# RWKV attention and a routed expert layer: attention by steps of 64 tokens on quarters of the array

## The chip, the cores and the metric

The kernel runs on one core of a Trainium2 chip. A core has a matrix engine (PE, whose weight loads are listed apart as PEld), a vector engine (DVE), a scalar engine (ACT), a general engine (POOL) and an engine that issues transfers (SP). Each runs its own stream of instructions in order, and they meet at semaphores. 16 DMA engines move data between HBM and the core's memory SBUF; PE writes its results to PSUM, 8 banks of 512 fp32 numbers in each of 128 partitions. The metric is the time of one execution in microseconds on the device; the median of three runs counts.

## The reference

Two blocks in a row. First an attention with a decaying state, for 4 batches, 8 heads, 768 tokens, 48 numbers per head:

```python
for t in range(S):
    kt, vt, rt = (k[:, :, t], v[:, :, t], r[:, :, t])
    cur = np.einsum('bhd,bhe->bhde', u[None] * kt, vt)
    y[:, :, t] = np.einsum('bhd,bhde->bhe', rt, state + cur)
    state = w[None, :, :, None] * state + np.einsum('bhd,bhe->bhde', kt, vt)
```

The term with `u` is a token's own term: the sum over d of r, u and k of this token, times v. Its outputs, laid side by side, are rows x of 384 numbers. Then a mixture of experts: 9 logits per token (8 experts and one gate that says whether the token keeps the expert of the token before it), and for each token one expert of 384 x 1024 x 384 with a relu between, scaled by the softmax's probability. All of it is in fp32.

## The kernel before

The attention works on 16 items; an item is one batch and one pair of heads (`M = B * HP`). Head 0 of the pair lies in partitions 0 to 47, head 1 in 64 to 111. The tokens of an item are cut into 6 chunks of 128 (`NCH`). Within a chunk the decay is moved into r and k: `rw` is r times a rising power of w, `kw` is k times the inverse power, so that their product gives the weights between tokens of a chunk. From chunk to chunk a state is carried.

Per item these steps are written, and each engine takes its part of them in this order (method `run`, lines 343 to 472):

- `load` (193): SP issues three transfers, `rk` (r and k turned, 768 KB), `kv` (k and v by tokens, 584 KB) and `vT` (v turned, 384 KB). They are issued three items ahead, each when its buffer is free.
- `scale` (207), on POOL: `ke` (k weighed for the chunk's end, two instructions), `rw` (two) and `pd` (r times k, two). `keys` (235), on DVE: `kw`.
- `scores` (273): 24 products, weights `kw` of 64 tokens of one head, moving `rw` of 128 or 64 tokens, into a pair of PSUM banks; DVE multiplies them with a mask into `am` (288), in two halves.
- `own` (260): 4 products of 384 columns with `u` as weights sum `pd` over d into `y`; DVE multiplies by `vT` in place (271).
- `added` (244): 10 products of all 128 tokens of a chunk into `T`, one per chunk and head. `states` (253): one scan on DVE over `T` gives the states.
- `inside` (290) and `before` (299), for the item before: 12 products with v as weights and `am` moving, and 10 with the state as weights and `rw` moving, added to `y`. The outputs have d along the partitions, so ACT copies them to `xT` (312) and `turn` (315) turns them: 6 transposes on PE and two ACT copies to `x`, which goes to HBM once per batch (326).
- `logits` (328) and `token_logits` (337), once per batch: 8 products of 384 columns from `xT`, then 3 that bring tokens to the partitions.

The first three items are written in an order of their own. From item 8 on (`g`) the router of the first two batches is spread over the items; item 15 issues the first gathers of rows for the experts. Then `Experts.run` (1274 on) takes over: `hidden` (1061) is the first product of the experts, and from there on PE runs the 10 blocks of rows. The first expert's weights are fetched by SP during item 14.

A product in fp32 is recorded twice in the trace, a pass each, and each pass has a weight load of its own. PE's four quarters (upper or lower half of the partitions in, upper or lower half out) can hold products of their own.

Of the kernel before, what the change touches and what calls it, by code (L numbers as in the profile page):

```python
# [1 line left out]

# [9 lines left out]
F32 = mybir.dt.float32  # L12
# [37 lines left out]
C2 = NCH // 2  # L50
AHEAD = 4
VB = NCH * 2 * DH

# [7 lines left out]
class Attention:  # L61
# [12 lines left out]

    def __init__(self, tc, st, rk_d, kv_d, vT_d, x_d, w_t, wp_d, kept, ident, lt, mp):
        self.tc, self.nc = tc, tc.nc
        nc = tc.nc
        self.rk_d, self.kv_d, self.vT_d, self.x_d = rk_d, kv_d, vT_d, x_d
        self.w_t, self.kept, self.ident, self.lt = w_t, kept, ident, lt

        self.late = st.enter_context(tc.tile_pool(name="late", bufs=1))
        self.wp = self.late.tile([P, H, 32], F32, name="wp")
        self.sel = self.late.tile([P, 2 * (E + 1)], F32, name="sel")
# [13 lines left out]
        self.T = mp[:, 2 * P + 2:2 * P + 2 + (NCH - 1) * DH].rearrange("p (e c) -> p e c", c=NCH - 1)  # L97

        self.inv = pool("pinv", 1, space=PSUM).tile([P, HP, P], F32, name="inv")
# [3 lines left out]
        self.rks, self.vTs = [None] * AHEAD, [None] * AHEAD  # L103
        for i in range(1, AHEAD + 1):
            self.rks[(n + i) % AHEAD] = once.tile([P, 2, NCH, P], F32, name=f"rk{i}")
        for i in range(1, AHEAD + 1):
            self.vTs[(n + i) % AHEAD] = once.tile([P, 2, C2, P], F32, name=f"vT{i}")
        self.kvs = [once.tile([P, 2 * VB + DP - DH], F32, name=f"kv{i}") for i in range(AHEAD + 1)]
        self.items = [dict() for _ in range(B * HP)]
        self.xTs, self.xs, self.lTs = {}, {}, {}  # L110
        for i in range(AHEAD - 1):
            self.load(i)
        nc.sync.dma_start(out=self.wp, in_=wp_d)


        self.step = once.tile([P, HP, DH, NCH - 1], F32, name="step")
        nc.vector.memset(self.step, 0.0)


        self.tab = tab = once.tile([P, HP, 2, P + 1], F32, name="tab")  # L120
# [8 lines left out]
        while n <= P:  # L129
            m = min(n - 1, P + 1 - n)  # L130
            for engine, t in ((nc.vector, tab[:, :1]), (nc.gpsimd, tab[:, 1:])):
                engine.tensor_mul(t[..., n:n + m], t[..., 1:1 + m], t[..., n - 1:n].to_broadcast([P, t.shape[1], 2, m]))
            n += m

        self.first, self.newton = mp[:, :P + 1], mp[:, P + 1:2 * P + 1]
        nc.scalar.copy(self.first, tab[:, 0, 0])
        self.reciprocals(0)

        self.end = once.tile([P, HP, P + DP], F32, name="end")
        self.endT = once.tile([P, 2, HP, 2 * DH], F32, name="endT")  # L140
# [12 lines left out]
    def reciprocals(self, i):  # L153

        nc, inv = self.nc, self.tab[:, i, 1, 1:]
        nc.vector.scalar_tensor_tensor(self.newton, self.first[:, 1:], -1.0, inv, Alu.mult, Alu.mult)
        nc.vector.scalar_tensor_tensor(self.inv[:, i], self.newton, 2.0, inv, Alu.add, Alu.mult)

# [6 lines left out]
    def ends(self, z):  # L165
        self.nc.scalar.copy(self.end[:, z, :P], self.tab[:, z, 0, P - 1::-1])
        self.nc.scalar.copy(self.end[:, z, P:], self.tab[:, z, 0, P - 1:DP - 1:-1])  # L167

    def turn_ends(self, z):
        ep, n = self.banks("ep"), z.stop - z.start  # L170
        for k in range(n):
            for o in range(2):
                self.nc.tensor.transpose(ep[:, o, k * P:(k + 1) * P], self.end[:, z.start + k, o * DP:o * DP + P], self.ident)
        self.nc.scalar.copy(self.endT[:, :, z].rearrange("p o i (h d) -> p o (i h) d", h=2),
                            ep[:, :, :n * P].rearrange("p o (i d) -> p o i d", d=DP)[..., :DH])

    def tables(self):

        nc, tab = self.nc, self.tab
        self.ends(slice(1, HP))  # L180
        for i in range(HP):
            nc.scalar.copy(self.step[:, i, :, 1:], spread(tab[:, i, 0, P:].to_broadcast([P, NCH - 2]), 1, DH))

    def chooser(self):

        self.nc.vector.tensor_reduce(self.sel, self.ident.rearrange("p (j i) -> p i j", j=4)[:, :2 * (E + 1)], axis=AX.X, op=Alu.add)
# [6 lines left out]
    def load(self, n):  # L193
        nc = self.nc
        b, hp = divmod(n, HP)
        rk, vT, kv = self.rks[n % AHEAD], self.vTs[n % AHEAD], self.kvs[n % (AHEAD + 1)]
        if n:
            nc.sync.dma_start(out=rk.rearrange("p a c t -> p (a c t)"), in_=self.rk_d[b, hp])
        else:
            for z in (slice(0, C2), slice(C2, NCH)):  # L200
                nc.sync.dma_start(out=rk[:, :, z], in_=self.rk_d[b, hp].rearrange("p (a c t) -> p a c t", a=2, c=NCH)[:, :, z])
        nc.sync.dma_start(out=kv, in_=self.kv_d[b, hp])
        nc.sync.dma_start(out=vT.rearrange("p a c t -> p (a c t)"), in_=self.vT_d[b, hp])
        self.items[n].update(b=b, hp=hp, rT=rk[:, 0], kT=rk[:, 1], vT=vT,
                             k=kv[:, :VB].rearrange("p (c x) -> p c x", c=NCH), v=kv[:, VB:])

    def scale(self, n):

        nc, t = self.nc, self.items[n]
        t["ke"] = self.two.tile([P, NCH, 2 * DH], F32, name="ke")  # L210
        t["pd"] = self.two.tile([P, NCH, P], F32, name="pd")
        t["rw"] = self.three.tile([P, NCH, P], F32, name="rw")
        hp = t["hp"]

        def ke(p):
            nc.gpsimd.tensor_mul(t["ke"][:, p::2], t["k"][:, p::2], spread(self.endT[:, p, hp], 1, C2))  # L216

        def pd(i):
            z = slice(i * C2, (i + 1) * C2)
            nc.gpsimd.tensor_mul(t["pd"][:, z], t["rT"][:, z], t["kT"][:, z])  # L220

        def rw(i):
            self.decayed(nc.gpsimd, n, slice(i * C2, (i + 1) * C2))

# [1302 lines left out]
```

## Time and profile before

| | us |
|---|---|
| median of 3 runs | 399.98 (399.34 to 401.64) |
| profiled execution | 398.36 |
| its span | 396.57 |
| first expert product (L1061) starts at | 119.34 |
| PE / PEld busy | 382.4 / 298.0 |
| DVE / POOL / ACT busy | 190.4 / 144.5 / 81.1 |
| data by SP's queue q1 | 56.89 MB |

The table of slices shows PE at 90% or more in nearly every fortieth of the span, a granted clock of full speed, and the DMA engines at 90% or more in the first six slices (60 us), at some 410 GB/s. "Issue" in the lists of waits is time in which an engine stood still and nothing that the profile shows held it. A stretch line gives for each engine the busy time and in brackets the number of instructions, in the order PE, PEld, DVE, ACT, POOL, then granted clock, DMA share and GB/s. A queue line gives packets, MB, and the share of the 16 engines' time.

### The profile page before, as it was taken

How to read it: one execution, taken by the hardware profiler on the slowest of the kernel's cores; microseconds unless marked ns; L12 is line 12 of the kernel's file. 1: busy time of each engine (PE TensorE's matmuls, PEld its weight loads, DVE VectorE, ACT ScalarE, POOL GpSimd, SP SyncE). 2: the span in 40 equal slices, each digit the busy share in tenths (PEclk: the TensorE clock that was granted, in tenths of full speed). 3: DMA queues.
4: the chain of work that ended last, by engine and by line, in shares of the span. 5: the costliest groups of instructions: out<-in, count | busy, mean ns of one | idle time of the engine just before them, and what ended most of it. 6: DMA issues, size and time to landing. Idle time of an engine off the chain costs nothing. (4 is left out here: it accounts for less than half of the span.)

```text
span 396.6 us, 8820 instructions
## 1 busy us (share of the span) xinstructions
PE 382.4 (96%) x3616; PEld 298.0 (75%) x3616; DVE 190.4 (48%) x533; ACT 81.1 (20%) x195; POOL 144.5 (36%) x179
## 2 busy tenths in 40 slices
PE   7999999999999999999999999999999999999992
PEld 6777777786769998666777787777767767779971
DVE  7887575778844743553432353255244244230200
ACT  4132222222222111111311121130031030131110
POOL 8679998887140052001633034014013023020012
PEclk9999999999999999999999999999999999999998
DMA  7999997998026774600842182073165064072011
GB/s 251 412 412 406 411 395 260 366 313 352 10 61 222 295 310 124 260 1 21 304 176 65 21 321 88 10 262 136 34 218 193 2 231 169 2 275 95 2 36 35
DMA packets 17473, 74.94 MB, mean 189 GB/s; under 512 B 2735, under 2 KB 6592, under 8 KB 14865
## 3 DMA queue, kind: packets, MB, share of 16 engines
q1 hardware_dynamic: 10048, 56.89, 38.5%
q0 software_dynamic: 3424, 9.54, 7.3%
q10 hardware_dynamic: 3952, 7.87, 5.3%
q8 instruction: 30, 0.49, 0.5%
q14 instruction: 19, 0.15, 0.1%
HBM read 64.85 MB, written 9.54 MB: 188 GB/s over the span
## 5 line engine op out<-in xcount | busy, mean ns | idle before, releaser
L1061 PE MATMUL h<-exT,w1t 128*128 128x192 f32 (+7 forms) x480 | 137.3, 428 | 1.0 <-ACT hT L1066 1.0
L1061 PEld LDWEIGHTS h<-exT,w1t 128*128 128x128 f32 x480 | 85.9, 190 | 33.9 <-issue 13.1
L1177 POOL DMA_INDIRECT out_dram<-yo,sid x27 | 27.6, 1021 | 183.2 <-ACT yo L1172 104.1
L1048 DVE COPY exT<-tp 128x384 f32<-128x384 f32 (+7 forms) x29 | 14.2, 494 | 96.6 <-PE tp L1047 96.6
L1066 ACT ACTIVATE hT<-h 128x192 f32<-128x192 f32 (+6 forms) x64 | 27.3, 428 | 142.6 <-PE h L1061 136.2
L1034 POOL DMA_INDIRECT xg<-x_d,gid x29 | 30.1, 1037 | 45.7 <-DVE sm L873 25.8
L288 DVE TENSOR_TENSOR am<-pair,kept 128x768 f32<-128x768 f32 x32 | 30.1, 952 | 16.3 <-PE pair L286 15.7
L220 POOL TENSOR_TENSOR pd<-rk 128x384 f32<-128x384 f32 x32 | 31.7, 1010 | 3.3 <-DMA rk<-in_rk_dram 2.5
L1074 PE MATMUL y<-hT,w2t 128*128 128x192 f32 (+1 forms) x144 | 29.1, 339 | 0.0
L295 PE MATMUL y<-am,kv 128*64 128x128 f32 x384 | 27.8, 278 | 1.1 <-DVE y L271 0.6
L1106 PE MATMUL y<-factors,sums 128*128 128x192 f32 x144 | 27.3, 326 | 0.0
L216 POOL TENSOR_TENSOR ke<-kv,endT 128x288 f32<-128x288 f32 x32 | 24.9, 796 | 4.6 <-DMA kv<-in_kv_dram 3.5
L233 POOL TENSOR_TENSOR rw<-rk,tab 128x384 f32<-128x384 f32 x26 | 23.5, 923 | 6.1 <-PE y L308 6.1
L295 PEld LDWEIGHTS y<-am,kv 128*64 128x64 f32 x384 | 23.9, 136 | 2.2 <-DVE y L271 1.2
L1074 PEld LDWEIGHTS y<-hT,w2t 128*128 128x128 f32 x144 | 25.0, 190 | 0.5
L1106 PEld LDWEIGHTS y<-factors,sums 128*128 128x128 f32 x144 | 24.1, 190 | 0.0
L286 PE MATMUL pair<-rw,kw 48*64 48x128 f32 (+1 forms) x768 | 22.5, 248 | 1.0 <-ACT end L167 0.6
L286 PEld LDWEIGHTS pair<-rw,kw 48*64 48x64 f32 x768 | 19.4, 133 | 2.4 <-ACT end L167 0.8
L312 ACT COPY xT<-y 128x768 f32<-128x768 f32 (+1 forms) x16 | 12.5, 779 | 40.9 <-PE y L308 40.9
L1113 PE MATMUL tp<-w2t,hT 128*120 128x384 f32 (+2 forms) x48 | 19.6, 490 | 0.0
L1106 PE MATMUL y<-w2t,hT 128*128 128x192 f32 x80 | 19.5, 326 | 0.0
L1106 PEld LDWEIGHTS y<-w2t,hT 128*128 128x128 f32 x80 | 14.2, 190 | 7.0 <-issue 2.7
(255 smaller groups left out, 496.5 us busy)
## 6 DMA issues: line engine op xcount, KB each, us to landing
w1t<-in_w_dram SPq DMA_DIRECT2D x9, 1536.0 KB, 6.2
w2t<-in_w_dram SPq DMA_DIRECT2D x9, 1536.0 KB, 8.9
rk<-in_rk_dram SPq DMA_DIRECT2D x15, 768.0 KB, 9.5
kv<-in_kv_dram SPq DMA_DIRECT2D x16, 584.0 KB, 9.9
vT<-in_vT_dram SPq DMA_DIRECT2D x16, 384.0 KB, 8.3
x_d<-x ACTq DMA_DIRECT2D x4, 1152.0 KB, 9.7
w1t<-in_w_dram ACTq DMA_DIRECT2D x1, 1536.0 KB, 9.3
w2t<-in_w_dram ACTq DMA_DIRECT2D x1, 1536.0 KB, 12.6
```

Source lines behind the costliest of these rows:

```text
L216: nc.gpsimd.tensor_mul(t["ke"][:, p::2], t["k"][:, p::2], spread(self.endT[:, p, hp], 1, C2))
L220: nc.gpsimd.tensor_mul(t["pd"][:, z], t["rT"][:, z], t["kT"][:, z])
L233: engine.tensor_mul(t["rw"][:, z], t["rT"][:, z], spread(pw, 1, z.stop - z.start))
L286: nc.tensor.matmul(sc[f * DP:(f + 1) * DP, h, i, x:], lhsT=t["kw"][q, c, o * DP:(o + 1) * DP], rhs=t["rw"][q, c, x:], start=True, stop=True)
L288: return lambda: nc.vector.tensor_mul(t["am"][:, g], sc, spread(self.kept[:, g:g + 3], 1, 2))
L295: nc.tensor.matmul(t["y"][p * DP:(p + 1) * DP, h, c2 * P:(c2 + 1) * P], lhsT=t["v"][:, (2 * c + h) * DH:(2 * c + h) * DH + DP], rhs=t["am" ...
L1034: self.nc.gpsimd.indirect_dma_start(out=xg[:n], out_offset=None, in_=self.x_d[:rows], in_offset=bass.IndirectOffsetOnAxis(ap=u["gid"][:n, ...
L1061: nc.tensor.matmul(h[:, :n], lhsT=u["w1"][:, m, kk, :], rhs=u["xT"][:, kk, :], start=(kk == 0), stop=(kk == DK - 1))
L1066: nc.scalar.activation(u[m], h[:, :n], Act.Relu)
L1074: nc.tensor.matmul(u["y"][d][:, :n], lhsT=u["w2"][:, m, d * P:(d + 1) * P], rhs=u[m], start=(m == 0), stop=(m == FK - 1))
L1106: nc.tensor.matmul(bank[:, x * half:(x + 1) * half], lhsT=a, rhs=b, start=(j == 0 and x == 0), stop=(j == FK // 2 - 1), skip_group_check=True)
L1177: self.nc.gpsimd.indirect_dma_start(out=out.rearrange("n (h d) -> (n h) d", h=2) if half else out, out_offset=bass.IndirectOffsetOnAxis(ap ...
```

## The change

The step becomes 64 tokens (`L`), so the state is carried 12 times per item, and every product of the attention is 64 by 64 in one quarter of the array (`quarter`). The own term is no longer a sum over `pd`: ACT multiplies k by u (`weighed`), PE forms all products of r and u k of a step (`own_terms`), and DVE keeps the diagonal in `am`; the weights between tokens of a step are then copied over it where a mask allows (`scores`, one predicated copy). `vT` and `pd` are gone. `added` makes a contribution for each of the 64-token steps; the first step is weighed for the end of the second (`k0`, `end0`), so that one scan of 480 elements carries 10 states, and ACT forms the one after the first step (`second`). `inside` and `before` now have `am` and `rw` as weights and v and the state (48 columns) moving, so that outputs have tokens along the partitions and ACT copies them straight to `x`. Two generators are drawn from in turn (`together`), so that the products of `added` of one item alternate with those of `inside` of the item before. Between `inside` and `before` ACT reads one column of `y` (`between`), which orders the two. `turn` now makes `xT` from `x`, for the logits alone, three groups of 6 transposes per batch; the logits are 18 products per batch with tokens along the partitions from the start. The router's steps are spread anew over items 10 to 15. From item 11 on, POOL does half of `kw`. At the start the tables are half as long. Of the expert part only PSUM's division is changed (a second bank of transposes is shared with `T`), and the order of the last batch's logits ahead of the first expert.

```diff
+L = P // 2
...
+STEPS = 2 * NCH - 2
...
@@ -193,155 +199,184 @@
     def load(self, n):
         nc = self.nc
         b, hp = divmod(n, HP)
...
+        rk, kv = self.rks[n % AHEAD], self.kvs[n % (AHEAD + 1)]
         if n:
             nc.sync.dma_start(out=rk.rearrange("p a c t -> p (a c t)"), in_=self.rk_d[b, hp])
         else:
             for z in (slice(0, C2), slice(C2, NCH)):
                 nc.sync.dma_start(out=rk[:, :, z], in_=self.rk_d[b, hp].rearrange("p (a c t) -> p a c t", a=2, c=NCH)[:, :, z])
         nc.sync.dma_start(out=kv, in_=self.kv_d[b, hp])
...
+        self.items[n].update(b=b, hp=hp, rT=rk[:, 0], kT=rk[:, 1],
                              k=kv[:, :VB].rearrange("p (c x) -> p c x", c=NCH), v=kv[:, VB:])
...
+    def decayed(self, engine, n, z):
+        t = self.items[n]
+        pw = self.tab[:, t["hp"], 0, :L] if n else self.first[:, :L]
+        if "rw" not in t:
+            t["rw"] = self.three.tile([P, NCH, 2, L], F32, name="rw")
+        c = z.stop - z.start
+        engine.tensor_mul(t["rw"][:, z], t["rT"][:, z].rearrange("p c (o t) -> p c o t", o=2), spread(spread(pw, 1, 2), 1, c))
+    def keys(self, engine, n, z):
+        t = self.items[n]
+        if "kw" not in t:
+            t["kw"] = self.two.tile([P, NCH, 2, L], F32, name="kw")
+        inv = (self.inv if engine is self.nc.vector else self.inverse)[:, t["hp"]]
+        c = z.stop - z.start
+        engine.tensor_mul(t["kw"][:, z], t["kT"][:, z].rearrange("p c (o t) -> p c o t", o=2), spread(spread(inv, 1, 2), 1, c))
+    def weighed(self, n):
+        t = self.items[n]
+        t["uk"] = self.two.tile([P, NCH, P], F32, name="uk")
+        for z in self.halves(n):
+            self.nc.scalar.activation(t["uk"][:, z], t["kT"][:, z], Act.Copy, scale=self.w_t[:, t["hp"], 1:2])
+    def ended(self, n):
+        nc, t = self.nc, self.items[n]
+        t["ke"] = self.kes[n % 2]
+        ke = t["ke"][:, :NCH * 2 * DH].rearrange("p (c x) -> p c x", c=NCH)
+        for z in (slice(0, C2), slice(C2, NCH)):
+            nc.gpsimd.tensor_mul(ke[:, z], t["k"][:, z], spread(self.endT[:, t["hp"]], 1, C2))
+        t["k0"] = self.k0s[n % 2]
+        nc.gpsimd.tensor_mul(t["k0"][:, :2 * DH], t["k"][:, 0], self.end0T[:, t["hp"]])
     def scale(self, n):
...
+        self.ended(n)
+        for z in (slice(0, C2), slice(C2, NCH)):
+            self.decayed(self.nc.gpsimd, n, z)
+    def quarter(self, out, lhsT, rhs, **kw):
+        return self.nc.tensor.matmul(out, lhsT=lhsT, rhs=rhs, skip_group_check=True, **kw)
+    def products(self, name, a, b):
+        sc = self.banks(name)
+        for c in range(NCH):
             for o in range(2):
                 for h in range(2):
...
+                    q, f = slice(h * DP, h * DP + DH), h ^ o
+                    self.quarter(sc[f * L:(f + 1) * L, h, c * L:(c + 1) * L], a[q, c, o], b[q, c, o], start=True, stop=True)
+        return sc[:, :, :NCH * L].rearrange("p h (c t) -> p h c t", c=NCH)
+    def own_terms(self, n):
+        t = self.items[n]
+        r, uk = [x.rearrange("p c (o t) -> p c o t", o=2) for x in (t["rT"], t["uk"])]
+        sc = self.products("ow", uk, r)
+        t["am"] = self.two.tile([P, 2, NCH, L], F32, name="am")
+        self.nc.vector.tensor_mul(t["am"], sc, spread(spread(self.own, 1, NCH), 1, 2))
+    def scores(self, n):
+        t = self.items[n]
+        sc = self.products("sc", t["kw"], t["rw"])
+        self.nc.vector.copy_predicated(t["am"], spread(spread(self.kept, 1, NCH), 1, 2), sc)
+    def added(self, n, o):
+        t = self.items[n]
+        def product(ke, c, h, i):
+            x = (2 * c + h) * DH
+            q = slice((o ^ h) * L, (o ^ h) * L + L)
+            self.quarter(self.T[h * DP:(h + 1) * DP, :, i], ke[q, x:x + DP], t["v"][q, x:x + DH], start=ke is t["k0"], stop=True)
+        for c in range(NCH):
+            i = 2 * c + o - 1
+            if i < STEPS:
+                for h in range(2):
+                    product(*((t["ke"], c, h, i) if i >= 0 else (t["k0"], 0, h, 0)))
+                yield
+    def second(self, n):
+        t = self.items[n]
+        t["S1"] = self.two.tile([P, DH], F32, name="S1")
+        self.nc.scalar.activation(t["S1"], self.T[:, :, 0], Act.Copy, scale=self.inverse[:, t["hp"], L - 1:])
+    def states(self, n):
         nc, t = self.nc, self.items[n]
+        S = self.two.tile([P, DH, STEPS], F32, name="S")
+        t["S"] = [t["S1"]] + [S[:, :, i] for i in range(STEPS)]
+        nc.vector.tensor_tensor_scan(S.rearrange("p e c -> p (e c)"), self.step[:, t["hp"]].rearrange("p e c -> p (e c)"),
+                                     self.T.rearrange("p e c -> p (e c)"), 0.0, Alu.mult, Alu.add)
+    def inside(self, n, h):
+        t = self.items[n]
+        if h:
+            t["y"] = self.py.tile([P, 2, 512], F32, name="y")
         for c in range(NCH):
...
+            x, z = (2 * c + h) * DH, c * DH
+            for o in range(2):
+                q = slice((o ^ h) * L, (o ^ h) * L + L)
+                self.quarter(t["y"][o * L:(o + 1) * L, h, z:z + DH], t["am"][q, h, c], t["v"][q, x:x + DH],
+                             start=c == 0, stop=False)
+            yield
+    def together(self, *parts):
+        for _ in zip_longest(*parts):
+            pass
     def before(self, n):
...
+        for c in range(NCH):
+            z = c * DH
+            for o in range(2):
+                for h in range(2):
+                    q = slice(h * DP, h * DP + DH)
+                    if c or o:
+                        self.quarter(t["y"][o * L:(o + 1) * L, h, z:z + DH], t["rw"][q, c, o],
+                                     t["S"][2 * c + o - 1][q], start=False, stop=True)
+        x = self.xs[b].rearrange("p c (h e) -> p h c e", h=H)
+        for h in (1, 0):
+            y = t["y"][:, h, :NCH * DH].rearrange("p (c e) -> p c e", c=NCH)
+            (nc.vector.tensor_copy if h == 0 and n == B * HP - 1 else nc.scalar.copy)(x[:, 2 * hp + h], y)
+        if hp == HP - 1:
+            nc.scalar.dma_start(out=self.x_d[b * S:(b + 1) * S, :].rearrange("(c p) d -> p c d", p=P), in_=self.xs[b])
+    def between(self, n):
+        self.nc.scalar.copy(self.none, self.items[n]["y"][:, :, 0])
+    def turn(self, b, k, banks):
+        nc = self.nc
+        for c in range(NCH):
+            z = slice(c % C2 * P, (c % C2 + 1) * P)
+            nc.tensor.transpose(banks[c // C2][:, z], self.xs[b][:, c, k * P:(k + 1) * P], self.ident)
+        xT = self.xTs[b][:, k].rearrange("p (g t) -> p g t", g=2)
+        for g in range(2):
+            (nc.vector.tensor_copy if g and b == B - 1 and k == DK - 1 else nc.scalar.copy)(xT[:, g], banks[g][:, :C2 * P])
+    def logits(self, b, bank, ks):
+        n = E + 1
+        for k in ks:
+            for c in range(NCH):
+                self.nc.tensor.matmul(bank[:, c * n:(c + 1) * n], lhsT=self.xTs[b][:, k, c * P:(c + 1) * P], rhs=self.wg[:, k],
+                                      start=(k == 0 and c == 0), stop=(k == DK - 1), skip_group_check=True)
+        if ks[-1] == DK - 1:
+            self.nc.scalar.copy(self.lt[:, b * NCH:(b + 1) * NCH, :].rearrange("p c e -> p (c e)"), bank[:, :NCH * n])
     def run(self, router, fetch, heads):
+        nc = self.nc
         def pair(name):
             t = self.banks(name)
...
             if n + AHEAD - 1 < M:
                 self.load(n + AHEAD - 1)
             elif n + 2 == M:
                 fetch()
+            if n < M:
+                self.own_terms(n)
...
             if n == 0:
...
+                self.ends(slice(1, HP))
                 self.turn_ends(slice(1, HP))
...
+                self.steps(slice(1, HP))
+                self.scores(0)
+            self.together(*([self.added(n, 0)] if n < M else []), *([self.inside(n - 1, 1)] if n else []))
             if n < M:
...
+                self.second(n)
+            if n + 1 < M:
+                self.weighed(n + 1)
+            if 0 < n < M:
+                self.scores(n)
...
+            self.together(*([self.added(n, 1)] if n < M else []), *([self.inside(n - 1, 0)] if n else []))
             if n < M:
                 self.states(n)
...
+            if n:
+                self.between(n - 1)
+            b, k = divmod(n - 2, HP)
+            if n >= 2 and k:
+                self.turn(b, k - 1, pair("tp"))
+            elif n > 2:
+                self.logits(b - 1, pair("lp")[0], range(DK))
...
             if n + 1 < M:
+                shared = n > g + 2
+                self.keys(nc.vector, n + 1, lo if shared else slice(0, NCH))
+                if shared:
+                    self.keys(nc.gpsimd, n + 1, hi)
                 self.scale(n + 1)
...
+            if n:
+                self.before(n - 1)
...
```

## The prediction

> **What bounds the kernel now.** I read the page first: PE is busy 96% of the span, so PE's own stream has to be explained, and the end follows from it. The steps that the change touches lie ahead of the first product of the experts (L1061, 119.34 us in the timeline); from there to the end is 277.2 us of expert work that the change leaves alone. So the question is when that first product can start.
>
> The timeline of PE shows one item (two heads of one batch, 768 tokens) in steady state:
>
> ```profile
> 80.97 0.79 PE L308 MATMUL y<-rw,S 48*48 48x128 f32 x18
> 81.61 1.27 PE L286 MATMUL pair<-rw,kw 48*64 48x128 f32 x46
> 82.86 0.88 PE L267 MATMUL y<-pd,w_t 48*64 48x384 f32 x8
> 83.67 0.88 PE L321 MATMUL pair<-ident,xT 128*128 128x128 f32 x6
> 84.47 0.79 PE L251 MATMUL mp<-kv,ke 128*64 128x48 f32 x20
> ```
>
> From start to start: L308 0.64, L286 1.25, L267 0.81, L321 0.80, L251 0.72, and L295 before them 1.51: 5.7 us of products per item. PE seems the bound. But the counts say something else. Ten products of L308 give 20 records: each fp32 product is two passes, and each pass is a weight load and a product, four instructions. Then there are places where PE stands still and waits for nothing that the profile shows, "issue":
>
> ```profile
> 58.48 0.46 PE L308 MATMUL y<-rw,S 48*48 48x128 f32 x3
> 60.18 0.70 PE L308 MATMUL y<-rw,S 48*48 48x128 f32 x17 [1.24 <-issue]
> ```
>
> The table of stretches, cut at the ends of such stalls (8.31 is a block's beginning reckoned back), counts the instructions between them (PE, then PEld):
>
> ```profile
> 8.31:60.17 51.86, 49.59 (x1012) 38.70 (x1013) 38.93 (x74) 13.12 (x34) 45.87 (x62) 1.00 1.02 406
> 33.85:52.88 19.02, 19.02 (x378) 14.52 (x378) 13.20 (x34) 5.62 (x17) 19.02 (x29) 1.00 1.03 412
> 52.88:60.17 7.29, 6.05 (x127) 4.77 (x126) 4.20 (x5) 1.50 (x3) 7.29 (x9) 1.00 0.99 372
> 60.17:73.35 13.18, 12.82 (x252) 9.28 (x252) 9.14 (x16) 3.68 (x8) 11.27 (x14) 1.00 0.85 299
> ```
>
> 756, 253 and 504, and with 12, 3 and 8 semaphore waits in PE's stream 768, 256 and 512. PE stops at multiples of 256 instructions. The page's queues say why:
>
> ```profile
> q1 hardware_dynamic: 10048, 56.89, 38.5%
> q8 instruction: 30, 0.49, 0.5%
> ```
>
> 0.49 MB in 30 packets is 16 KB each, 256 instructions of 64 bytes: PE's program comes in blocks over the same DMA engines as the data. Narrow DMA views place the packets. They end at 32.50, 51.36, 58.59 and 72.02 us; PE goes on at 33.86, 52.89, 60.18 and 73.36, 1.3 to 1.6 us later each time. A packet starts some time after PE has entered the block before it: entered at 52.89, started 57.65, 4.8 us, while q1 filled the engines (the share is about 1.0 until 60 us); 3.6 and 4.4 us for the two blocks entered at 60.18 and 66.69; but 0.4 us for those entered at 79.47 and 85.38, and 0.7 to 0.9 after 98 us. So one block costs PE at least wait + 1.0 (packet) + 1.4 (to resume): 2.8 to 3.3 us when data transfers are out of the way, 6 to 7 us when not (52.89 to 60.18 is 7.29). **Today one item is 264 instructions for its 66 products and takes 6 to 7 us, hardly faster than its fetch.**
>
> The Trainium skill ("Runtime: NRT & Kernel Launch", Instruction fetch mechanics) knows the blocks of 256 instructions, but says that crossing a boundary is mostly hidden. By it the sum below has no fetch and ends near 389 us. The 1.24 us row above contradicts it here, and the trace decides.
>
> **The change, part by part.** *Products.* Per item 66 products (24 scores, 4 own, 10 added, 12 inside, 10 before, 6 transposes) become 24 own, 24 scores, 22 added, 24 inside, 22 before, which is 116 in quarters, and in three items of four 6 transposes. Their time on the array: L308 and L286 pass 1280 columns in 0.64 us and 2304 in 1.25 us, 1.9 columns per ns with four quarters alternating. A 48-column pass is no shorter than a 64-column one (L251: ten steps in 0.72 us for 48 columns). So 116 x 64 / 1.9 = 3.9 us; 3.3 if every quarter keeps a 57 ns step (L151: 52 passes on one part of the array in 2.98 us), 6.7 if L251's 58 ns per product held. I take 3.9, since L286 is the nearest kind. With a transpose group (L321 0.80, and 0.1 for the switch of shape) 4.8 against today's 5.7. *Instructions:* 116 x 4 + 12 and some waits = 480 against 264. That is the change's real price.
>
> *Logits.* L334 with L340 (1.5 + 0.8 us) give way to 18 products with a 128-column weight: 36 passes at L340's 0.11 us = 4.1 us, 72 instructions, once per four items (+1.8 us of PE each).
>
> *DVE.* Loses L271 (0.96) and one L288 (0.95), gains the diagonal's multiply (0.95, as L288) and the predicated copy (no row; 0.95 as L288, 1.9 if it takes two passes), and the scan doubles to 480 elements: L257's 645 ns for 240 and L722's 376 for 104 give 2 ns each, 1.14. With kw 0.95: 4.0 us per item against 4.5 (5.0 with the dear copy). Still under the fetch. *ACT:* uk 0.8, second state and the small ordering copy 0.2 each, x copies 2 x 0.4, xT copies 2 x 0.48: 3 us. *POOL:* ke 2 x 0.8, k0 0.4, rw 2 x 0.93, later half of kw 0.93: 3.9 to 4.8 against 5.4 (pd is gone). *DMA:* vT's 384 KB of 1736 go, 6.3 MB, 15 us of transfer at 410 GB/s; they come back only as shorter waits of the fetch. SP loses one issue per item; the gate's weights go from SP's queue to ACT's, 14 KB at the start: nothing. New waits: the copy ahead of `before` holds PE for an ACT round, but a transpose group or the logits lie between, 0.7 us for 0.4 (without them own(n+1) stands behind it, and DVE's multiply behind that: 0.4 per item); added(n) waits for the scan, own(n+1) covers it. I count these at nothing while fetch leads; without fetch they make 4.8 into about 5.1.
>
> A rule speaks against the pairs of added and inside: the skill's "TensorEngine Tiling (Array Packing)", Gotcha 1, says that row tiles cannot use the same PSUM bank at once. Here two row halves write one bank, at different partitions. No row of before does that. If each pair went in turn, 46 products would cost 1.3 us more per item, mostly under the fetch.
>
> **The sum.** Instructions up to the first expert product: today 2215 + 2216 records in 0 to 119.34 us and 67 waits, 17.6 blocks. After, from the order of the built program: 1856 quarter products and 113 others at four, 102 transposes at two, 70 waits = 8150, 31.8 blocks. PE enters its second block in own(0), near 7.9 us; 30.8 blocks follow. 3 blocks meet the loads of the first four items (5.4 MB, 13 us at 410 GB/s): 6 us each, 18. For the other 27.8: 3.0 with free engines, plus waiting. rk and kv of an item are issued apart, 1.9 and 1.5 us of transfer; a request in one waits half of it on average: (1.9² + 1.5²)/2 per 7 us = 0.4. Three stores of x (3.3 us each) and the first weights (3 MB, 7.5 us) catch some six requests for 2 us, 0.4 per block. 27.8 x 3.8 = 106. The three batches of logits inside keep PE longer than their fetch, 1 us each: 3. Sum 7.9 + 18 + 106 + 3 = 135 us, 15.6 later than 119.34. The profiled execution takes 398.36 us (span 396.6), so 414; the median shown is 1.6 above it: **415 us**. Bounds of the wait: 0.4 to 2.0 per block beyond the start: 2.8 gives 107 us (388), 4.4 gives 151 (432); with 1 us more for slower quarters at the few places where PE leads, up to 440.
>
> **Rivals.** *Faster: fetch stays hidden* (waits like the 0.4 us at 79.47 everywhere, with q1 then moving some 350 GB/s). Then PE's 5.1 per item leads: second item at 14.5 us (POOL's first ke and rw), fifteen steps x 5.1 + 3 x 3.3 for logits, 7 until the first expert product: 108 us, 389. For it: vT's bytes are gone. Against it: two blocks per item, and a request at 92.3 waited 3 us behind one weight load. 17%. *Tie:* 3.3 us per block, 119 to 121 us, 400: 6%. *Much slower: every request finds a backlog* as between 27 and 67 us, 5.5 per block: 177 us, 458; against it, each transfer is now issued when PE frees a buffer, and 1352 KB need 3.4 us of a 7 us item. 7%. *The change doesn't do what it says:* the quarters don't overlap, 0.114 us per product, 13 us per item, 520 us; L308's rate speaks against it, 1%. Forecast: 69%.
>
> The range is 388 to 440, which leaves out the lower half of the first rival and the last two; the likeliest case's own is 403 to 430. A measurement here tells 0.5% (2 us) from no change. Faster 0.19 (rival one and the lower end of the forecast's waits), same 0.06, slower 0.75.
>
> **What would show it.** Right: some 44 packets on q8 instead of 30; PE and PEld counts between issue stalls again in 256s; PE idle on "issue" tens of us in the first 135 us, landing in whatever line is next; DVE and POOL less busy per item. First expert product at 127 to 150 us. Wrong: no issue stalls and waits on kw, rw or the scan instead (rival one); predicated copy near 2 us with PE waiting on DVE; stalls inside added and inside that are no block ends (bank rule).

## The result and the profile after

| | before | after |
|---|---|---|
| median, us | 400.46 (4 runs) | 460.06 (4 runs, 456.01 to 463.11) |
| ratio, 95% interval | | 1.1454 [1.1355, 1.1554] |
| span of the profiled execution, us | 396.57 | 454.1 |
| first expert product (L1061), us | 119.34 | 169.25 |
| from there to the end, us | 277.2 | 284.8 |

The change makes the kernel 14.5% slower; the run of 463.11 us, over 1.5% above the fastest, is left out of the ratio. Of the 57.5 us between the two spans, 49.9 arise ahead of the first expert product and 7.6 behind it. The page of the changed kernel, the lines that answer to those of before:

```profile
span 454.1 us, 12463 instructions
PE 409.9 (90%) x5435; PEld 339.3 (75%) x5435; DVE 180.0 (40%) x504; ACT 98.1 (22%) x250; POOL 127.6 (28%) x176
...
PEclk9678967876887867999999999999999999999999
...
q1 hardware_dynamic: 7600, 50.47, 30.8%
...
q8 instruction: 45, 0.74, 0.7%
...
L283 DVE COPY_PREDICATED am<-kept,pair 128x768 f32<-128x768 int32 x16 | 16.4, 1022 | 30.8 <-PE pair L259 30.8
```

45 packets of instructions instead of 30, less data, and the predicated copy takes 1.02 us: all as reckoned. New is the line PEclk, the granted clock. Now 14 of the first 16 slices (182 us) hold six to eight; before the change it read

```profile
PEclk9999999999999999999999999999999999999998
```

The waits of PE in the first 150 us (total, times, longest):

```profile
PE pair L259 <- issue: 12.0, 7, 3.4
PE y L259 <- issue: 10.5, 6, 3.0
PE mp L259 <- DVE pos L725: 1.8, 1, 1.8
```

PE waits mostly for its own instructions: 22.5 us, against some 9 us for all other engines together, none of those waits over 1.8 us. The timeline of PE shows a batch's logits and one such stall:

```profile
59.21 1.25 PE L259 MATMUL pair<-rw,kw 48*64 48x64 f32 x48
61.02 6.30 PE L372 MATMUL pair<-wg,xT 128*128 128x9 f32 x36
67.26 1.41 PE L259 MATMUL y<-S,rw 48*64 48x48 f32 x42
...
93.59 1.23 PE L259 MATMUL pair<-rk,uk 48*64 48x64 f32 x35 [3.33 <-issue]
```

and the table of stretches, cut where the clock changes (the column of two decimals behind the engines is the granted clock):

```profile
59.34:62.76 3.42, 3.39 (x112) 3.19 (x108) 2.21 (x3) 1.28 (x3) 1.82 (x3) 1.00 0.83 270
62.76:73.00 10.24, 10.24 (x236) 10.21 (x240) 1.88 (x3) 2.62 (x11) 2.04 (x3) 0.50 0.29 91
73.00:79.82 6.82, 4.84 (x220) 4.37 (x215) 3.63 (x4) 2.84 (x7) 3.59 (x5) 1.00 0.72 241
90.06:93.48 3.42, 0.21 (x11) 0.13 (x5) 0.45 (x1) 0.70 (x2) 1.68 (x2) 1.00 1.06 408
93.48:96.89 3.41, 3.30 (x124) 3.29 (x127) 0.96 (x1) 0.83 (x2) 0.00 (x0) 0.50 0.37 91
```

The logits begin at full clock and end at half. The stretch 90.06 to 93.48, in which PE stood for its instructions while data filled the DMA engines (1.06), is followed by 3.41 us at half clock. 72.4 us of the first 169.25 pass at half clock.

### The profile page after: what moved, and what is told of

It reads as the page before. It is cut to its first block, busy times and chain, and to the rows that moved or that the text cites. A ratio compares the mean times of both kernels' runs of the same rounds, so it can differ in the third digit from the quotient of the medians.

```text
span 454.1 us, 12463 instructions
## 1 busy us (share of the span) xinstructions
PE 409.9 (90%) x5435; PEld 339.3 (75%) x5435; DVE 180.0 (40%) x504; ACT 98.1 (22%) x250; POOL 127.6 (28%) x176
## 5 line engine op out<-in xcount | busy, mean ns | idle before, releaser
L1061 PE MATMUL h<-exT,w1t 128*128 128x192 f32 (+7 forms) x480 | 139.2, 434 | 1.0 <-ACT hT L1066 1.0
L1061 PEld LDWEIGHTS h<-exT,w1t 128*128 128x128 f32 x480 | 87.9, 194 | 34.1 <-issue 13.3
L1066 ACT ACTIVATE hT<-h 128x192 f32<-128x192 f32 (+6 forms) x64 | 27.3, 428 | 149.0 <-PE h L1061 145.7
L259 PE MATMUL y<-kv,am 64*64 64x48 f32 x768 | 37.1, 249 | 7.5 <-issue 7.5
L259 PEld LDWEIGHTS y<-kv,am 64*64 64x64 f32 x768 | 33.1, 164 | 8.8 <-issue 8.1
L259 PE MATMUL mp<-kv,ke 64*64 64x48 f32 x640 | 31.9, 249 | 4.4 <-DVE pos L725 1.8
L259 PEld LDWEIGHTS mp<-kv,ke 64*64 64x64 f32 x640 | 28.7, 166 | 5.1 <-issue 1.9
L277 DVE TENSOR_TENSOR am<-pair,own 128x768 f32<-128x768 f32 x16 | 15.3, 958 | 35.0 <-PE pair L259 35.0
L283 DVE COPY_PREDICATED am<-kept,pair 128x768 f32<-128x768 int32 x16 | 16.4, 1022 | 30.8 <-PE pair L259 30.8
L1074 PEld LDWEIGHTS y<-hT,w2t 128*128 128x128 f32 x144 | 26.2, 198 | 2.7 <-ACT hT L1066 2.2
L259 PE MATMUL pair<-rw,kw 48*64 48x64 f32 x768 | 21.0, 255 | 7.7 <-issue 7.7
L1106 PE MATMUL y<-factors,sums 128*128 128x192 f32 x144 | 27.3, 326 | 0.0
L259 PE MATMUL pair<-rk,uk 48*64 48x64 f32 x768 | 21.9, 266 | 4.8 <-issue 4.3
L259 PE MATMUL y<-S,rw 48*64 48x48 f32 x704 | 22.0, 279 | 4.1 <-issue 3.0
L259 PEld LDWEIGHTS pair<-rk,uk 48*64 48x64 f32 x768 | 20.0, 176 | 5.6 <-issue 4.7
```

Source lines behind the costliest of these rows:

```text
L259: return self.nc.tensor.matmul(out, lhsT=lhsT, rhs=rhs, skip_group_check=True, **kw)
L277: self.nc.vector.tensor_mul(t["am"], sc, spread(spread(self.own, 1, NCH), 1, 2))
L283: self.nc.vector.copy_predicated(t["am"], spread(spread(self.kept, 1, NCH), 1, 2), sc)
L1061: nc.tensor.matmul(h[:, :n], lhsT=u["w1"][:, m, kk, :], rhs=u["xT"][:, kk, :], start=(kk == 0), stop=(kk == DK - 1))
L1066: nc.scalar.activation(u[m], h[:, :n], Act.Relu)
L1074: nc.tensor.matmul(u["y"][d][:, :n], lhsT=u["w2"][:, m, d * P:(d + 1) * P], rhs=u[m], start=(m == 0), stop=(m == FK - 1))
```

## The experiments

Each comparison has its own runs of the kernel before, on the same chip; chips differ by up to 1.4%, so the ratios are compared. The first theory: PE lacks instructions, and the clock falls where the array has streamed few columns.

**Phases of PE alone.** A kernel of its own, phases one behind the other.

> A kernel of its own: it computes nothing of the reference and writes zeros; PE runs phases one after the other, fp32, set apart by full products (128x128 weights, 512 columns). (1) 640 quarter products of 64x64 weights and 64 columns, the layout of the changed kernel, no data transfer beside them; (2) the same with 128 columns; (3) 54 products with 128x128 weights and 9 columns, as the logits; (4) six times five groups of 6 full products, each group held up by a copy on VectorE that grows by 512 elements from one set to the next; (5) phase 1 again while 26 loads of 786 KB fill the DMA engines. Theory (PE is short of instructions, and the granted clock falls to half where the array has streamed few columns, whether it stood still or worked on 9 columns): phase 1 is 10 blocks of 256 instructions at 2.8 to 3.3 us, 28 to 33 us, with stalls near 1 us at the block ends and the clock at 1.0; phase 2 43 us (1.9 columns per ns), no stalls, clock 1.0; phase 3 starts at full clock and falls to half within 7 us, 17 to 22 us in all; in phase 4 the clock halves only in the sets with the longest waits; phase 5 45 to 60 us, stalls of 2 to 4 us and half clock in part of it. Rival (quarter products by themselves lower the clock): half clock in phases 1 and 2, over 40 and over 80 us. Rival (9 columns don't matter to the clock): phase 3 takes 12 us at clock 1.0. Rival (fetch is limited by its own latency, data do not matter): phase 5 takes what phase 1 takes.

Its timeline (the phases in order; the last two lines are phase 5):

```profile
33.16 2.09 PE L72 MATMUL pair<-a 48*64 48x64 f32 x128 [1.32 <-issue]
36.89 2.48 PE L72 MATMUL pair<-a 48*64 48x64 f32 x128 [1.64 <-issue]
...
84.36 35.63 PE L72 MATMUL pair<-a 48*64 48x128 f32 x1280
...
142.34 18.23 PE L77 MATMUL thin<-wide,a 128*128 128x9 f32 x108
...
476.27 3.69 PE L72 MATMUL pair<-a 48*64 48x64 f32 x128 [2.24 <-issue]
...
487.84 3.69 PE L72 MATMUL pair<-a 48*64 48x64 f32 x128 [2.78 <-issue]
```

and stretches of it (phase 2, phase 3 in two parts, phase 5):

```profile
84.40:119.90 35.50, 35.49 (x1281) 35.05 (x1280) 0.00 (x0) 0.00 (x0) 0.00 (x0) 1.00 0.02 4
142.34:147.62 5.28, 5.28 (x49) 5.27 (x48) 0.00 (x0) 0.00 (x0) 0.00 (x0) 1.00 0.00 0
147.62:160.40 12.78, 12.78 (x62) 12.78 (x62) 0.00 (x0) 0.00 (x0) 0.00 (x0) 0.50 0.00 1
465.30:505.80 40.50, 25.78 (x896) 24.46 (x896) 0.00 (x0) 0.00 (x0) 0.00 (x0) 0.50 1.02 393
```

With no data moving, 256 instructions take 3.45 us: the packet starts 1.1 us after PE entered the block before, takes 1.0, and PE goes on 1.4 later. 64 quarter products need only 2.09 us, so at full clock PE stalls at every block. In phase 1 the clock still alternated (half for two stretches of 6.8 us in 34), a miss; the loop stayed at 3.45 us there, so where the fetch sets the pace half clock costs nothing. Phase 2 has no stall, and the clock stays full: small quarters alone don't lower it. It took 35.6 us where 43 were expected. Phase 3 falls to half after 5.3 us. With loads running a block takes 5.1 to 6.5 us, all at half clock. Phase 4 kept the full clock with waits of up to 1.85 us behind 5.4 us of work; with 2.38 us and more it halved in most rounds (four of five at 2.38).

**The logits undone in the changed kernel.**

```diff
-for k in ks:                      # 18 products, 9 columns move
-    for c in range(NCH):
-        matmul(bank[:, c * n:(c + 1) * n], lhsT=xT[:, k, c * P:(c + 1) * P], rhs=wg[:, k])
+for k in range(DK):               # 6 products, 384 columns move
+    for g in range(2):
+        j = 2 * g + k % 2
+        matmul(bank[32 * j:32 * j + 32, :C2 * P], lhsT=wp[:, k, g], rhs=xT[:, k, g * C2 * P:(g + 1) * C2 * P])
+for j in range(C2):               # and 3 that turn them
+    matmul(bank2[:, j * n2:(j + 1) * n2], lhsT=lT[:, j * P:(j + 1) * P], rhs=sel)
```

> The changed kernel with one part undone: the logits. The tokens are the moving operand again (6 products of 384 columns on column groups and 3 products that turn them, per batch) instead of 18 products that move 9 columns against a 128x128 weight. Theory (the 9-column products lower the clock): the four batches fall from 6.4 us to about 2.5 us each and the half-clock stretches that begin at 62.8, 100.3, 141.3 and 161.7 us go; some of it is lost again, since the fetch of about one block per batch was hidden behind the logits: 12 to 20 us faster than the changed kernel, 438 to 446 us, mean clock over 0.93. Rival (the quarter products and the stalls alone lower the clock): 4 x 2 us = 8 us at most, 450 us or more, and half clock for about as long as before the edit.

443.82 us, ratio 1.1016 [1.0935, 1.1098] against the change's 1.1454: 16 us less by the medians, 17.5 by the ratios, as expected. The mean clock is 0.924, a little under the forecast: the stretches behind the logits went, but others came. Half clock ahead of the first expert product fell from 72.4 to 64.9 us only; in this the rival was right. Two lines of its timeline, a batch's logits:

```profile
62.83 1.49 PE L379 MATMUL pair<-xT,wp 128*32 128x384 f32 x12
...
65.89 0.84 PE L386 MATMUL pair<-sel,lT 128*128 128x18 f32 x6
```

2.3 us of products instead of 6.3. The experiments named "aw" below start from this variant.

**The logits' products alone, in the kernel before.**

```diff
+for i in range(18):                # 9 columns move, into columns that nothing reads
+    z = slice(C2 * P + i % 6 * 9, C2 * P + i % 6 * 9 + 9)
+    matmul(bank[:, z], lhsT=ident, rhs=ident[:, :9])
```

> The kernel before the change with the suspected part alone added: behind each batch's logits 18 more products of a 128x128 weight with 9 columns, into columns that nothing reads (4 x 72 instructions). Theory (products that stream few columns lower the clock): each block costs 6.3 us or so and leaves half clock behind it for some us more; 4 x (6.3 + 2) = 33, less the 3.5 us of stalls that they hide: 424 to 436 us, with three to four half-clock stretches of 7 to 14 us. Rival (their time is only the 0.11 us per pass that the forecast took): 4 x 4 = 16 us, 412 to 418 us, clock 1.0 throughout.

431.07 us, ratio 1.0675 [1.0597, 1.0754], inside the theory's range. The stretches around the first batch show it:

```profile
30.00:40.00 10.00, 9.39 (x164) 7.36 (x162) 6.73 (x8) 1.50 (x3) 10.00 (x17) 1.00 1.03 408
...
40.57:50.81 10.24, 10.24 (x91) 9.45 (x93) 1.25 (x20) 1.39 (x4) 5.97 (x10) 0.50 0.82 316
```

PE is busy throughout, and the clock halves for 10.24 us.

**More instructions at the same columns, in the kernel before.** A first build gave each of the own term's cut products a start flag of its own; with it the outputs changed, and the kernel's second, general path ran behind the first (L1376 and L1381, most of the 2848 us), so its time tells nothing. With the flag on the first piece alone:

```diff
-matmul(sc[..., x:], lhsT=kw, rhs=rw[q, c, x:])
+for z in (slice(x, x + m), slice(x + m, P)):   # m = (P - x) // 2; likewise inside, before, own
+    matmul(sc[..., z], lhsT=kw, rhs=rw[q, c, z])
```

> The kernel before the change with the number of instructions alone raised: each product of the scores, of the inner term and of the earlier states is cut into two of half the columns, the 4 of the own term into 12 of 128 columns; 66 products per item become 118, the result and every other engine's work stay. Theory (the instruction stream is short): about 31 blocks instead of 17.6 to the first expert product; at the 3.45 us per block that the phase without data took, and 5 to 6 while the loads of the first items run, that product starts at 140 to 160 us instead of 119.3 and the kernel takes 421 to 441 us, with 20 to 30 us of stalls at block ends (3.5 before) and half-clock stretches. Rival (the new layout, the other engines or the smaller quarters made the time, not the count): within 1% of the kernel before, 399 to 408 us.

459.35 us, ratio 1.1526 [1.1444, 1.1607], as slow as the change itself; 44 packets, 15.9 us of stalls. The sign is the theory's, the size is a miss, because the cut costs array time too: the 24 passes of the inner term took 1.51 us, the 48 of half the columns 2.05 (start to start, both at full clock). So this run doesn't show the price of the count by itself; the next one is the cleaner test.

**Fewer instructions at the same columns, in the changed kernel.**

```diff
-for c in range(NCH):
+for c in range(0, NCH, 2):         # likewise added, inside, before
     for o in range(2):
         for h in range(2):
-            quarter(sc[.., c * L:(c + 1) * L], a[q, c, o], b[q, c, o])
+            quarter(sc[.., c * L:(c + 2) * L], a[q, c, o], b[q, c:c + 2, o])
```

> The mirror of the kernel with the cut products: the variant with wide logits, and its quarter products joined in twos, one weight for the columns of two neighbouring chunks. 116 products per item become 64, nearly the same columns pass the array, 268 instructions instead of 476; every other engine's work, the loads and the quarters stay. The joined products use the first chunk's weights for both, so the outputs are not the reference's, and the test for overflow is set to zero so that no second path is taken. Theory (the instruction stream sets the time before the experts): 18 blocks instead of 31 to the first expert product, which starts at 100 to 118 us instead of 160.8; 378 to 396 us, below the kernel before; stalls at block ends under 8 us in all. Rival (VectorE, GpSimd, the waits between engines or the data set the pace of 8 us per item): above 425 us.

399.71 us, ratio 0.9969 [0.9947, 0.9991]: 9.5% less, by the ratios, than the variant it starts from, by a change of PE's products and their weight loads alone. The first expert product starts at 120.55 us; that and the time lie just outside the forecast. Half clock fell along with the stalls (27.3 us instead of 64.9), so the run doesn't tell the two apart. Its page:

```profile
PEclk9698999978989999999999999999999999999997
...
q8 instruction: 31, 0.51, 0.5%
```

**The loads left out.**

```diff
-dma_start(out=rk, in_=rk_d[b, hp]); dma_start(out=kv, in_=kv_d[b, hp])
+if n <= AHEAD:                     # the first five items only
+    dma_start(out=rk, in_=rk_d[b, hp]); dma_start(out=kv, in_=kv_d[b, hp])
```

> The variant with wide logits, with the loads of rk and kv left out from the sixth item on: the last eleven items compute on the data of earlier ones (their results are not the reference's, and the test for overflow is set to zero so that no second path is taken); the instructions of PE and the work of every engine stay. Theory (fetched blocks wait behind data packets): the block loop falls to the 3.45 us of the phase without data after the first 25 us, so the first expert product starts at 120 to 130 us instead of 150.2 and the kernel takes 411 to 422 us; stalls at the block ends remain, of about 1 us each. Rival (the fetch has its own latency and data do not matter, or PE waits on other engines): 145 us or more, 438 us or more. Rival (without data the fetch is hidden): below 115 us and no stalls.

421.17 us, ratio 1.0583 [1.0528, 1.0639]. (The 150.2 us of the expectation is the value of `b_thin`; the variant's own first expert product starts at 160.80, so the forecast of that point was too early and the one of the time held.) The product starts at 140.81, 20 us earlier: the loads cost that much, 12.1 us of it in stalls, and half clock is 13.7 us shorter. Even so it is 21 us later than in the kernel before.

**Loads three deep.** `AHEAD = 3` instead of 4.

> The variant with wide logits, its items loaded three deep instead of four: two items instead of three are requested at the start, and each later load one item later. The work is the same. Theory (a block waits behind the packets of the loads queued ahead of it): the backlog of the first 20 us shrinks by one item's 1352 KB (3.4 us), so the blocks fetched there come 2 to 5 us earlier in sum, 439 to 443 us. Rival (the order of the loads is no matter to the fetch, or the items now come late): no change within 0.5%, or slower by 1 to 3 us.

> The kernel before the change, its items loaded three deep instead of four. Theory (the stalls of 3.5 us there come from blocks queued behind loads): up to 3 us faster, 397 to 400 us against the 400.5 of the kernel before. Rival (items come late, since 1736 KB need 4.3 us of a 6 us item): 0 to 6 us slower.

In the changed design it gives 432.07 us, ratio 1.0880 [1.0822, 1.0937], more than expected: the first expert product moves from 160.80 to 151.17. In the kernel before it gives nothing, 1.0044 [1.0013, 1.0075], the rival's side.

**Work added on PE.**

```diff
+matmul(sc[:, 0], lhsT=ident, rhs=filler)    # 512 columns, ahead of own terms and of scores
```

> The variant with wide logits and work added on PE alone: ahead of each item's own terms and of its scores one full product of 512 columns into the bank that is overwritten next (0.87 us each at full clock, 8 instructions per item). Question: what the half clock costs by itself. If fetch alone sets the pace before the experts, PE has about 3 us per item to spare, the 1.7 us hide, the array streams enough to keep its clock (half-clock time before the experts below 25 us instead of 65), and the time stays within 1% of 443.8 (439 to 448). If the half clock costs by itself, it gets faster, 425 to 438. If PE's own work sets the pace, 16 x 1.7 = 28 us are added, 465 or more.

449.77 us, ratio 1.1204 [1.1150, 1.1259], between the answers. Half clock falls from 64.9 to 27.3 us and the stalls from 25.5 to 12.6. A fill takes 1.06 us from its start to the next product's at full clock, 32 x 1.06 = 34 us of work, yet the first expert product starts only 9.1 us later (169.9): the fill pays for most of itself. The stalls give back 12.9 us of the 34; some 12 are left for the half clock, which so seems to cost time by itself (argued, not shown apart).

**A fifth fewer instructions.** The own term by 4 products of 384 columns, in the variant three deep; then the same without the products of r and k.

```diff
-uk = k * u                                     # ScalarE
-24 x quarter(sc[64 rows, c], uk[q, c, o], r[q, c, o])
+pd = r * k                                     # half VectorE, half GpSimd
+4 x quarter(sc[64 rows, all c], u broadcast to 64, pd[q, o])    # aw_own4x: uk[q, o], no pd
```

> The variant with wide logits and three items ahead, its own term with a fifth of the instructions of an item less and the same result: r times k is multiplied on VectorE and GpSimd (half each; ScalarE's uk goes), and 4 products of 384 columns with u broadcast as the weight put every token's own value on all 64 rows, of which the diagonal's mask keeps one; 4 products take the place of 24, so 96 products and 396 instructions per item instead of 476. Theory (the number of instructions sets the time): 26 blocks instead of 31 to the first expert product; 5 x 4.4 = 22 us less, it starts at 128 to 138 us instead of 151.2; 1.02 to 1.05 times the kernel before, 410 to 420 us. Rival (GpSimd and VectorE, with 0.9 and 0.5 us more per item, set the pace): 1.07 times or more.

> The same 4 products in place of 24, but reading ScalarE's uk, which stays, so that GpSimd and VectorE have no product of r and k: only PE's instructions differ from the variant with three items ahead (its own term is not the reference's, and the test for overflow is set to zero so that no second path is taken). Theory (fewer instructions help, and it was the added 1.0 us on GpSimd and 0.85 us on VectorE per item, with the waits behind them, that gave it back): 26 blocks, first expert product at 128 to 140 us, 1.02 to 1.055 times the kernel before. Rival (a fifth fewer instructions is worth little at this count; something else, such as the waits between the engines, sets 8.3 us per item): first expert product at 148 us or later, 1.08 or more.

1.0992 [1.0915, 1.1069] and 1.0802 [1.0724, 1.0880]: both misses, the rivals' side each time. Blocks fell to 26 as reckoned, but the count alone gained under 1% here, within the intervals. So the first theory, in which the number of blocks sets the time, is incomplete. Adding up each trace up to its first expert product shows what it left out:

| | blocks | stalls at block ends S | half clock H | product starts T | T - S - H/2 |
|---|---|---|---|---|---|
| before | 17.6 | 2.7 | 0 | 119.3 | 116.7 |
| after | 31.8 | 25.6 | 72.4 | 169.2 | 107.4 |
| a_wide | 31.2 | 25.5 | 64.9 | 160.8 | 102.9 |
| aw_ahead3 | 31.2 | 20.9 | 54.6 | 151.2 | 102.9 |
| aw_quiet | 31.2 | 13.4 | 51.2 | 140.8 | 101.8 |
| aw_own4 | 26.2 | 18.8 | 71.7 | 158.4 | 103.8 |
| aw_own4x | 26.2 | 14.2 | 71.7 | 152.4 | 102.4 |
| aw_merge | 18.2 | 4.5 | 27.3 | 120.6 | 102.4 |

(us; S: standstills over 0.2 us, from one start to the next, where the count of instructions reaches a block's end. Half clock counts half, since the array's work there takes twice as long.) The last column is the same within 2 us over these six wide variants. A stall in half clock is counted in both prices; counted once, the column is 102.4 to 106.8. The seventh, `aw_fill`, fits less well: 169.9 - 12.6 - 27.3/2 = 143.7, and less its 34 us of fill 110. So stalls and half clock together make most of the difference between the variants. By this account half clock has 36.2 us in the changed kernel and the stalls 25.6, and `aw_own4x` against `aw_ahead3` saved 6.7 us of stalls and lost 8.6 by 17.1 us more of half clock.

The two prices hang together, though. Two runs of `aw_own4x` itself took 437.19 us at a mean clock of 0.908 (the one traced) and 432.48 at 0.945. By these clocks the first has some 33 us more of half clock, 16 us at the price above, but it is only 4.7 us longer. So H/2 is an upper bound of what full clock would give back; what each price is worth alone stays open.

**What sets the half clock.**

> A kernel of its own: it computes nothing of the reference and writes zeros; PE runs products of 512 columns without a pause, with no data transfers and few instructions, on parts of the array (rows x columns of the weight), each stretch of 24 to 30 products set apart by 24 full ones: 128x64, 64x64, 64x128, 128x32, 64x96, 32x32, 32x128. Theory, read from the 3.41 us stretches of the twelve traces so far: the clock of the next stretch is set by the columns streamed, each weighted with the share of the array that it uses; below about 1364 (a third of 4096) it is half. Full products stream 512 columns in 0.434 us, 4028 per stretch; so 128x64 (2014), 64x128 (2014) and 64x96 (1511) keep the full clock, 0.87 us per product; 64x64 (1007), 128x32 (1007), 32x128 (1007) and 32x32 (252) fall to half within 7 us, 1.74 us per product, though PE never stands still. Rival (only standing still lowers the clock, and the 9-column products did because of their weight loads): clock 1.0 in all seven.

Four of its seven phases in the timeline (rows * columns of the weight behind the tiles), and stretches of the second and of the sixth phase:

```profile
71.87 21.67 PE L82 MATMUL big<-wide,a 64*64 64x512 f32 x50
...
157.58 23.36 PE L82 MATMUL big<-wide,a 128*32 128x512 f32 x54
...
246.66 45.38 PE L82 MATMUL big<-wide,a 32*32 32x512 f32 x58
...
314.48 46.80 PE L82 MATMUL big<-wide,a 32*128 32x512 f32 x60
```

```profile
71.90:93.40 21.50, 21.50 (x51) 6.54 (x50) 0.00 (x0) 0.00 (x0) 1.00 0.00 0
252.00:291.00 39.00, 39.00 (x47) 7.79 (x45) 0.00 (x0) 0.00 (x0) 0.50 0.00 0
```

Five of seven as the theory said; 64x64 and 128x32 kept the full clock, so with one product at a time the columns of the weight don't count, while 32 rows halve it at 32 and at 128 columns. The rival falls as well: PE is busy 100% of the stretch at half clock. What fits all seven is columns streamed times rows fed.

## Why the prediction was wrong

It had the side right and one of two mechanisms, the fetch of PE's instructions; the half clock isn't in it. It was 45 us short, and its range ended at 440. By its own steps:

- *The bound and the count.* 31.8 blocks were forecast and 31.8 counted, 44 packets forecast and 45 seen, stalls sit at multiples of 256. Joining the products in twos brought the time back to that of the kernel before.
- *The first blocks.* 7.9 + 18 + 2 x 3.8 = 33.5 us for the start and five blocks; they took 32.95.
- *"27.8 x 3.8 = 106".* Here it failed. The 22 later blocks without logits took 4.47 us each, 14.8 us more in sum. Two things were short: the loop without data is 3.45 us, not 3.0 (phase 1), which makes up to 22 x 0.45 = 9.9 us of it, and "PE's work mostly under the fetch" holds at full clock only. At half clock 64 quarter products take 3.69 us instead of 2.09, and transposes and stalls come on top.
- *"36 passes at 0.11 us = 4.1 us" and "1 us each: 3".* The passes took 6.3 to 6.5 us, because 9 columns halve the clock. The three blocks with logits took 7.8, 8.2 and 8.8 us against 4.8 (+10.4). The last batch's logits and transposes had no time of their own in the sum: 13.1 us from the last full block to the first expert product, where 0.8 of a block, 3.0 us, was reckoned (+10.1).
- 14.8 + 10.4 + 10.1 less 0.5 is the distance from 134.5 to 169.25 us. The step behind much of it is one that the prediction didn't write down: every price was taken at full clock, since the trace of before shows no other up to the experts. There H is 0; after the change it is 72.4 us. Where stalls were forecast, the clock had to be asked for as well.
- *"Rest unchanged, 277.2".* It took 284.8. 9.6 us of it run at half clock (169.25 to 175.40 and 202.70 to 206.12), at most 4.8 us of the 7.6; the rest is open.
- *The edits at nothing.* They held: the predicated copy took 1.02 us (0.95 or 1.9 were the bounds), PE's waits for DVE and ACT are single ones under 2 us, and the bank rule doesn't show: at full clock a pass of added and inside, whose pairs share a bank, took 17 ns from start to start, one of the scores, whose row halves write different banks, 15.
- *The rivals.* "Much slower", 458, gave the right time by the wrong price: not 5.5 us per block but 4.5 and the logits. "Faster", 389, may be what the two prices hide: the column T - S - H/2 is 9 us lower after the change than before, 8 with each stall counted once (worked out, not run).

A version faster than the kernel before that computes the reference was not found; wide logits and loads three deep, 432.07 us, is the best such form of the changed design.

## What to carry to other kernels

Count instructions per microsecond of array time before cutting products into smaller ones. Without data in the way the fetch brought about 74 per us here (256 in 3.45 us; phase 2, at 72, had no stall), and under loads 39 to 50 (256 in 6.5 to 5.1 us). Wherever a change makes PE stall or move few columns, ask what the granted clock will do, and price the array's work behind it at half speed where the array and not the fetch sets the pace. Give the long side to the moving operand: 18 products of 9 columns per batch cost 16 to 18 us over a kernel in which 6 of 384 and 3 of 18 do the same.

## What the hardware showed unexpectedly

- **The granted clock follows what is fed to the array, not PE's busy time.** It changed in steps of 3.41 us. In the traces of twelve whole kernels (all but `b_split`), 1313 such stretches ran at full clock, and 74 of them were followed by one at half clock. One number tells them apart, the columns streamed in the stretch, each product weighted by the share of the array it used (full products stream 512 columns in 0.434 us, 4028 per stretch): with the border at 1364, 64 of the 74 lie below it and all of the 1239 others above. The stretches that halved fed up to 1536, those that didn't 1376 and more. `m_parts` shows that rows make this share and columns of the weight don't (64x64 alone stays full, 32x128 halves). For quarters in use side by side the two weights may come to the same; that wasn't tested. 64 quarter products of 54 columns feed 2 x 64 x 54 / 4 = 1728, so by this estimate a block that takes over 1728 / 1364 x 3.41 = 4.3 us ends at half clock; the changed kernel's took 4.47. Where in between 1007 and 2014 the border lies was not tried on its own; back to full clock the same number tells only 76% of 155 stretches.
- The Trainium skill ("TensorE: Matmul & The Clock Gate", Part 1) describes a clock that halves after a window of about 3.4 us without activity. The steps of 3.41 us agree; that idleness is needed does not, since 45 us of back-to-back products on 32 rows ran at half clock.
- The instruction loop: 3.45 us per 16 KB without data, 5.1 to 6.5 with the DMA engines full (phases 1 and 5).
- A pass over 128 rows with 64 columns is not half of one with 128: 24 passes of 128 columns took 1.51 us, 48 of 64 columns 2.05.
